# One row scatter per block at the end of attention, in a fused attention and mixture-of-experts kernel

## The chip, the cores and the metric

The kernel runs on one NeuronCore of one Trainium2 chip. The time is the device time of one execution in microseconds; the figure quoted is the median of the runs. Five engines work side by side, each through its own list of instructions in program order: TensorE (PE; its weight loads are shown apart, as PEld), VectorE (DVE), ScalarE (ACT), GpSimd (POOL) and SyncE (SP). POOL and SP also issue the DMAs.

## The reference

Two parts follow one another. The first is a gated attention over 8 sequences of 2816 tokens, whose queries and keys are the same array `z`, and whose scores go through a squared ReLU instead of a softmax:

```
scores = (1/S) * z @ z.T            # S = 2816, z has 64 columns
x = u * (max(scores, 0)**2 @ v)     # u, v: 256 columns
```

The second is a layer of 8 experts, of which each token uses one, beside a dense layer that all tokens use:

```
y = max(x @ w1_dense, 0) @ w2_dense
e = argmax(x @ w_gate);  g = softmax(x @ w_gate)[e]
y += g * (max(x @ w1[e], 0) @ w2[e])      # 256 -> 512 -> 256
```

There are 22528 tokens in all. The weights are small; which token goes to which expert is known only once its attention row is there.

## The kernel before

**Blocks.** The tokens are 176 blocks of 128. A sequence has 22 blocks. In attention, `av` (line 521) handles two blocks at a time: 22 key positions, two halves of each, and two blocks are 88 matmuls (line 548), with the score matmuls of later groups (line 383) put in between. ACT and DVE turn scores into the weights `A` (lines 398 to 413). Some of the weights are not computed but taken by DMA transpose from an earlier group (line 446, on SP). When a pair of blocks is done, DVE multiplies it by `u` and writes it to `pays` (line 577, `gate_x`), a ring of 22 blocks in SBUF. A DMA transpose of those rows (line 579) feeds the router.

**Routing and scatter.** The router works on groups of 11 blocks, at the end on groups of 8, 6, 4 and 4. `routing(q)` starts five blocks (`LAG`) after a group's last block: logits on PE (line 605), DVE's choice of expert (`route_a`), counts on PE (lines 635 and 636), and then positions in the expert's list (`route_b`), kept in `pos`. After that the blocks of the group stand in the list `waiting`. `one_scatter` takes the first of them: DVE casts the 128 positions to an index column `pi` (line 693), and POOL issues an indirect DMA that writes the block's 128 rows to the DRAM buffer `xs`, sorted by expert (line 695). This is called a row scatter below.

**The clock of the planner.** `tick(g)` runs once per block, in the middle and at the end of a pair; it does what was put down for that block with `at`, and then one row scatter. The order on PE, ACT, DVE and SP is fixed while the kernel is built, by a planner that keeps an estimated time `now` and the time at which each engine is free. For blocks after the first 154 (`Q1 * G`), `av` has a second call, in the middle of each half of a pair, so that up to two row scatters go out per block:

```
if x == nK // 2 and b * nK + i + p > Q1 * G:
    one_scatter()
```

**Tables.** When the first 14 groups (154 blocks) have their positions, `table(0)` works out, in ten steps on DVE, which rows each of the first 70 expert tiles takes, and of which expert it is. The steps are put down three to a block from block `t1` on. `table(1)` does the same for the rest, in the expert stage.

**Expert stage.** A tile is 256 rows of one expert, the last 22 are two halves of 128 rows. `fetch(s)` on SP reads a register from the table and loads the rows of `xs` by DMA transpose, then the gate and token numbers (lines 870 and 872). `expert(s)` copies that expert's weights on DVE (line 895). `slot(s)` is one step of the loop: 16 matmuls up (line 907) and 16 down (line 915), ReLU and a copy on ACT (lines 910 and 930), the weighted sum on DVE (line 931), and two scatters of finished rows to the output on POOL (line 933), called output scatters. After the first of them stands a copy on POOL that nobody reads (`pause`, line 920). DVE writes its sums in a ring of nine buffers, each of which is free when its output scatter has landed. Blocks still in `waiting` when attention ends are scattered here, one after every fifth slot, each with a pause of its own; they must all be out before the fetch of the 71st tile. The last two routing groups are routed in the first four slots.

The first three fetches are put down during the last blocks of attention, and `fetch(0)` may not start before the rows of the first 154 blocks are in `xs`. Rows of later blocks are declared independent of the first 70 tiles.

Of the kernel before, what the change touches and what calls it, by code (L numbers as in the profile page):

```python
# [19 lines left out]
def kernel(  # L20
# [19 lines left out]
    nK = S // P  # L40
    nB = N // P
    G = 11
# [5 lines left out]
    Q1 = nB // G - 2  # L48
# [35 lines left out]
    def banks(x, name, shape=(P, 2, 4 * P), dt=F32):  # L84

        return ps.tile(list(shape), dt, name=name, tag=f"b{x}")
# [179 lines left out]
    for b in range(B):  # L266
        i = 0
# [93 lines left out]
    def take_pair():  # L361
        return pairs.pop(0)[1]
# [73 lines left out]
    def far_steps(a):  # L436

        n = a + 2
        if n >= len(groups) or far[n] != [a]:
            return []  # L440
        (b, i0, w), (_, j0, wj) = groups[n], groups[a]

        def step(i):
            assert n - 1 in A
            open_group(n)
            nc.sync.dma_start_transpose(out=A[n][:, j0:j0 + wj, i * P:(i + 1) * P],
                                        in_=A[a][:, i0 + i, :wj * P])
            if i == w - 1:
                for j in range(wj):
                    key_at[n, j0 + j] = now[0] + 10.0  # L450

        return [(a, lambda i=i: step(i)) for i in range(w)]
# [68 lines left out]
    def av(n, i, between):  # L521
        b, i0, w = groups[n]
        if i == i0:
            turning.extend(far_steps(n))
        keep[0] = 0
        if n == 0 and i == i0:

            fill(n)
            for g in (0, 2):
                load_u(g, gate=True)  # L530
            need(n, 0)
        until(lambda: pairs[0][0] if pairs else None)
        ox = take_pair()
        o = banks(ox, "o")
        for p in range(2):
            rest = list(range(nK))
            for x in range(nK):
                k = rest[0]
                if i == i0 and p == 0:

                    k = min(rest, key=lambda k: (key_at.get((n, k), 9e9), k))
                    need(n, k)
                rest.remove(k)
                for h in range(2):
                    r = slice(h * dq, (h + 1) * dq)
                    j = p ^ h
                    c = (i + j - i0) * P
                    nc.tensor.matmul(out=o[:, j, 0:D], lhsT=A[n][r, k, c:c + P],  # L548
                                     rhs=v_of[b][r, k, :], start=(p == 0 and x == 0),
                                     stop=(p == 1 and x == nK - 1))  # L550
                pe(0.1092)
                keep[0] = 2 - p if x >= nK - 12 else 0
                if x % 2 == 1 and x < nK - 1:
                    fill(n)
                if x % 7 == 3 and turning:
                    t = can_turn(turning[0][0] + 2, turning[0][0])
                    if t is not None and t <= now[0] and turning[0][0] + 1 in A:
                        turning.pop(0)[1]()
                if x == nK // 2 and b * nK + i + p > Q1 * G:
                    one_scatter()  # L560
            if p == 0:
                swap_rows(n)
                between()

        def done(t):
            give_pair(t + 0.1, ox)

        g = b * nK + i
        offer(now[0] + 0.2, 0, {"dve": (0.63, lambda eng: gate_x(g, o))}, done)
        keep[0] = 0  # L570
# [13 lines left out]
    def vec(name, a, b=1, dt=F32, **kw):  # L584

        t = rt.tile([P, G * E if b > 1 else G], dt, name=name, **kw)
        return t[:, :a * b].rearrange("p (a b) -> p a b", b=b) if b > 1 else t[:, :a]
# [53 lines left out]
    def route_b(q):  # L641

        n = sizes[q]
        oh, ex, pre = rs[q]
        inc = vec("inc", E, n)

        def one():
            se = vec("se", n)
            nc.vector.tensor_reduce(out=se, in_=ex, axis=AX.X, op=ALU.add)
            o = starts[q] % (2 * G)  # L650
            rows = pays[:, o:o + n, :]
            nc.vector.reciprocal(rows.bitcast(F32)[:, :, P], se)
            nc.vector.tensor_copy(rows.bitcast(I32)[:, :, P + 1], tok[:, starts[q]:starts[q + 1]])
            assert q != Q1 or made_first[0]
            if first_of[0] != n:

                first_of[0] = n
                nc.vector.memset(smask[:, :E * n], 1.0)
                nc.vector.memset(smask[:, :E * n].rearrange("p (e t) -> p e t", e=E)[:, :, 0], 0.0)

        def two():
            tb = vec("tb", E, n)
            nc.vector.tensor_copy(tb, pre[0])
            nc.vector.tensor_add(tb[:, :, 0], tb[:, :, 0], base[:])
            nc.vector.tensor_tensor_scan(
                out=inc.rearrange("p e t -> p (e t)"), data0=smask[:, :E * n],
                data1=tb.rearrange("p e t -> p (e t)"),
                initial=0.0, op0=ALU.mult, op1=ALU.add)
            nc.vector.tensor_copy(base[:], inc[:, :, n - 1])

        def three():
            nc.vector.tensor_add(inc, inc, pre[1])
            nc.vector.tensor_mul(inc, inc, oh)
            pos = vec("pos", n, bufs=3)
            nc.vector.tensor_reduce(out=pos, in_=inc.rearrange("p e t -> p t e"),
                                    axis=AX.X, op=ALU.add)
            rs[q] = pos

        return [one, two, three]
# [179 lines left out]
    def fetch(s):  # L859

        x = take("x")
        me = mx.tile([P, 2, 2], F32, name="me", bufs=16)
        if s < NT1:
            R = nc.values_load(Rt[0][0:1, s:s + 1], engines=[ET.SP], min_val=0,
                               max_val=XROWS - T2,
                               skip_runtime_bounds_check_because="made by the table")
            xT = x.rearrange("p (c h t) -> p h c t", c=2, h=2)
            rows = xs[bass.ds(R, T2), :]
            for ins in (
                    nc.sync.dma_start_transpose(out=x.rearrange("p (c t) -> p c t", c=2),  # L870
                                                in_=rows.bitcast(BF)[:, 0:D]),
                    nc.sync.dma_start(out=me[:], in_=rows[:, P:P + 2].rearrange("(j p) c -> p j c", p=P))):

                nodep(ins, ["fx"], "xs2")
            return xT, me
        xT = x.rearrange("p (h c t) -> p h c t", c=2, h=2)
        k = 2 * (s - NT1)
        Rs = nc.values_load_multi_w_load_instructions(
            Rt[1][0:1, k:k + 2], engines=[ET.SP], min_val=0, max_val=XROWS - P,
            skip_runtime_bounds_check_because="made by the table")[1]  # L880
        for j in range(2):
            rows = xs[bass.ds(Rs[j], P), :]
            nc.sync.dma_start_transpose(out=xT[:, j], in_=rows.bitcast(BF)[:, 0:D])
            nc.sync.dma_start(out=me[:, j, :], in_=rows[:, P:P + 2])
        return xT, me
# [65 lines left out]
    got, wes = {}, {}  # L951
# [28 lines left out]
    def at(tick, fn):  # L980
        later.setdefault(tick, []).append(fn)
# [25 lines left out]
    waiting = []  # L1007
    placed = set()

    def one_scatter(dve=True):  # L1010
        if not waiting:
            return
        g = waiting.pop(0)
        if dve:
            offer(now[0], 0, {"dve": (0.1, lambda eng: scatter(g))}, lambda t: placed.add(g))
        else:
            scatter(g)
            placed.add(g)
# [47 lines left out]
    LAG = 5  # L1066
# [3 lines left out]
    for n, q in enumerate((nQ - 2, nQ - 1)):  # L1070
        at(nB + 2 * n, lambda q=q: late_routing(q))
        at(nB + 2 * n + 1, lambda q=q: late_places(q))
    t1 = Q1 * G + LAG + 2
    steps = table(0)
    for n, fn in enumerate(steps):
        at(t1 + n // 3, lambda n=n, fn=fn: offer(now[0], 0.5, {"dve": (0.7, lambda eng: fn())},
                                                 lambda t: made_first.__setitem__(0, n == len(steps) - 1)))
    fetched = [3]
    for s in range(fetched[0]):
        at(nB - 4 + s, lambda s=s: got.update({s: fetch(s)}))  # L1080
    at(nB - 2, lambda: wes.update({0: expert(0)}))
    t2 = nB + 10
    for n, fn in enumerate(table(1)):
# [21 lines left out]
    for s in range(NT - MAYBE + 2):  # L1105
        assert s + AHEAD < NT1 or not waiting
        slot(s, NT - MAYBE)
        for fn in later.pop(nB + s, []):
            fn()
        if s % 5 == 1 and waiting:  # L1110
            g = waiting[0]
            one_scatter(dve=False)
            pause(pays[:, g % (2 * G), 0:ROW].bitcast(F32))
    assert not waiting
    assert not later
    n = nc.values_load(used[0:1, 0:1], min_val=0, max_val=NH,
                       skip_runtime_bounds_check_because="made by the table")
# [34 lines left out]
```

## Time and profile before

| | |
|---|---|
| median of 3 runs | 930.4 us (929.56 to 930.82) |
| the profiled execution | 937.3 us, its span 935.5 us |
| mean granted TensorE clock | 0.987 |
| end of attention, first expert matmul | 582.7 us after the span's start |
| busy: PE, ACT, DVE, POOL | 95%, 79%, 75%, 52% of the span |
| row scatters, output scatters | 176, and 180 (40 of them for the last tiles) |

A row of the timeline gives start, duration, engine, line, operation, the tiles written and read, and in square brackets how long the engine was idle before it and what ended that. "Issue" is a wait for which the profile shows no cause, "remote" one that ended on something outside its records. A row of the windows gives the stretch and its length, the busy time and count of PE, PEld, DVE, ACT and POOL, then the granted clock, the share of the DMA engines and GB/s. A row of the waits gives who waited for whom, the total, how often, and the longest. A row of the chain gives start, length and what was running. A row of the groups gives line, engine, operation, tiles, count, busy time and mean ns, and the idle time just before it by cause.

### The profile page before, as it was taken

Reading aid. Unit: us, or ns where it says so; the run is one execution under the profiler, and the core shown is the slowest. Engines: PE = TensorE matmul, PEld = TensorE weight load, DVE = VectorE, ACT = ScalarE, POOL = GpSimd, SP = SyncE. Lnnn points to the kernel's source line nnn. Section 1 sums busy time; section 2 is a strip of 40 time slices with the busy share of each in tenths; the row PEclk is TensorE's granted clock in tenths of the full one; section 3 lists DMA queues with packets and bytes.
Section 4 is the critical chain, followed back from the end, with each engine's and each line's share of the span. In section 5 each row is a group of like instructions: output and inputs, shape, how many; then the busy total and the mean of one; then the engine's idle time right before and its main releaser. Section 6 shows DMA issues by size and latency. Waiting matters only on the chain.

```text
span 935.5 us, 30562 instructions
## 1 busy us (share of the span) xinstructions
PE 885.6 (95%) x12256; PEld 763.3 (82%) x12256; DVE 703.3 (75%) x1319; ACT 736.3 (79%) x913; POOL 489.7 (52%) x525
## 2 busy tenths in 40 slices
PE   8999999999999999999999997999899998999996
PEld 5898888888888888888887775878787887888785
DVE  6999989999999999989997972656454444446553
ACT  7999989998989989989988770667666667677664
POOL 7203343335345344344446434577777877877455
PEclk9999999999999999999999988999999999999999
DMA  7994995996997999998998745565444444434332
GB/s 139 152 181 102 164 184 112 175 200 132 178 191 133 190 179 141 193 177 142 189 188 133 140 88 91 111 123 121 100 106 106 111 111 107 117 103 95 87 91 72
DMA packets 257871, 127.64 MB, mean 136 GB/s; under 512 B 225470, under 2 KB 232894, under 8 KB 257728
## 3 DMA queue, kind: packets, MB, share of 16 engines
q1 hardware_dynamic: 230112, 70.24, 45.2%
q0 software_dynamic: 27616, 55.44, 27.7%
q8 instruction: 96, 1.57, 0.7%
q14 instruction: 47, 0.39, 0.2%
HBM read 61.54 MB, written 37.16 MB: 105 GB/s over the span
## 4 chain that ended last, share of the span: by engine, by line
PE 64%; POOL 14%; issue 12%; DVE 4%; DMA 3%; ACT 1%; POOLq 1%; SPq 0%; another core or an unknown queue 0%; DVEq 0%; ACTq 0%
PE o L548 41%; PE s L383 10%; POOL out_dram L933 9%; PE h_ps L907 6%; PE yy L915 6%; POOL zr L920 2%; DMA xT<-pays 2%; PE lg L605 1%; DVE r L400 1%; POOL A L413 1%; DVE A L413 1%; DVE ring L931 1%; DMA out_dram<-ring,ix 1%; DVE ring L895 1%; DVE pays L577 1%
## 5 line engine op out<-in xcount | busy, mean ns | idle before, releaser
L548 PE MATMUL o<-vb,A 64*128 64x256 bf16 x7744 | 501.2, 272 | 8.9 <-issue 6.0
L548 PEld LDWEIGHTS <-A 64*128 64x128 bf16 x7744 | 412.2, 95 | 62.6 <-issue 11.8
L695 POOL DMA_INDIRECT xs<-pays,pi x176 | 199.3, 1133 | 276.6 <-DVE pi L693 220.6
L398 ACT ACTIVATE r<-s 128x1024 f32<-128x1024 f32 x279 | 275.3, 1014 | 38.5 <-PE s L383 29.0
L910 ACT ACTIVATE ring<-h_ps 128x1024 bf16<-128x1024 f32 x180 | 185.6, 1032 | 95.3 <-PE h_ps L907 40.5
L411 ACT ACTIVATE A<-r 128x1024 bf16<-128x1024 f32 x252 | 256.5, 1044 | 1.7 <-DVE r L400 1.3
L413 DVE TENSOR_TENSOR A<-r 128x1024 bf16<-128x1024 f32 x172 | 208.2, 1223 | 1.1 <-ACT r L398 0.2
L931 DVE SCALAR_TENSOR_TENSOR ring<-yy,me,ring 128x256 f32<-128x256 f32 x180 | 86.1, 482 | 151.6 <-ACT ring L930 84.2
L400 DVE TENSOR_SCALAR r<-s 128x1024 f32<-128x1024 f32 (+1 forms) x153 | 185.0, 1216 | 12.3 <-PE s L383 8.3
L933 POOL DMA_INDIRECT out_dram<-ring,me x140 | 146.2, 1044 | 66.5 <-DVE ring L931 32.5
L915 PEld LDWEIGHTS <-ring 128*128 128x128 bf16 x1440 | 139.8, 98 | 38.6 <-issue 22.8
L383 PE MATMUL s<-zT 64*128 64x512 bf16 (+1 forms) x944 | 162.7, 364 | 7.1 <-remote 2.8
L915 PE MATMUL yy<-w2d,ring 128*128 128x256 bf16 x720 | 107.9, 272 | 17.3 <-DVE ring L931 15.3
L915 PE MATMUL yy<-ring 128*128 128x256 bf16 x720 | 108.0, 273 | 0.0
L907 PE MATMUL h_ps<-ring,w1d 128*128 128x256 bf16 x720 | 94.0, 273 | 3.0 <-ACT ring L910 1.3
L907 PE MATMUL h_ps<-ring 128*128 128x256 bf16 (+1 forms) x880 | 95.3, 253 | 1.4 <-issue 0.8
L895 DVE COPY ring<-wall 128x2048 bf16 x110 | 85.0, 788 | 10.4 <-issue 5.9
L930 ACT COPY ring<-yy 128x256 f32<-128x256 f32 x180 | 68.1, 378 | 30.3 <-PE yy L915 14.5
L907 PEld LDWEIGHTS <-ring 128*128 128x128 bf16 x880 | 73.4, 98 | 11.8 <-DVE ring L895 3.3
L577 DVE TENSOR_TENSOR pays<-o,ut 128x512 bf16<-128x512 f32 x88 | 61.2, 696 | 26.3 <-PE o L548 16.1
L907 PEld LDWEIGHTS <-w1d 128*128 128x128 bf16 x720 | 69.9, 98 | 12.3 <-issue 4.3
L383 PEld LDWEIGHTS <-zT 64*128 64x128 bf16 x944 | 58.5, 95 | 26.1 <-issue 15.2
(120 smaller groups left out, 359.3 us busy)
## 6 DMA issues: line engine op xcount, KB each, us to landing
ut<-in_u_dram SPq DMA_DIRECT2D x88, 256.0 KB
vb<-in_v_dram POOLq DMA_DIRECT2D x16, 384.0 KB
vb<-in_v_dram POOLq DMA_DIRECT2D x16, 320.0 KB
wall<-in_moe_w_dram POOLq DMA_DIRECT2D x16, 256.0 KB
xs<-pays,pi POOLq DMA_INDIRECT x176
zr<-in_z_dram POOLq DMA_DIRECT2D x7, 352.0 KB
out_dram<-ring,me POOLq DMA_INDIRECT x140
A<-A SPq DMA_TRANSPOSE x128
```

The source lines that it names most:

```text
L383: nc.tensor.matmul(out=s[:, h, y * c:(y + 1) * c], lhsT=zT[r, k + h, :], rhs=zT[r, i0:i0 + w, :], start=True, stop=True)
L398: nc.scalar.activation(r[:, :, :c], s[:, :, :c], AF.Relu, scale=1.0 / S)
L400: nc.vector.tensor_scalar(out=r[:, :, :c], in0=s[:, :, :c], scalar1=1.0 / S, scalar2=0.0, op0=ALU.mult, op1=ALU.max)
L411: nc.scalar.activation(a, r, AF.Square)
L413: (nc.gpsimd if eng == "pool" else nc.vector).tensor_mul(a, r, r)
L548: nc.tensor.matmul(out=o[:, j, 0:D], lhsT=A[n][r, k, c:c + P], rhs=v_of[b][r, k, :], start=(p == 0 and x == 0), stop=(p == 1 and x == nK - 1))
L695: ins = nc.gpsimd.indirect_dma_start(out=xs, out_offset=bass.IndirectOffsetOnAxis(ap=pi[:], axis=0), in_=pays[:, g % (2 * G), 0:ROW].bitca ...
L907: nc.tensor.matmul(out=h_ps[:, f, hs, :], lhsT=w1(c, f), rhs=xT[:, hs, c, :], start=(c == 0), stop=(c == 1))
L910: nc.scalar.activation(h, h_ps[:].rearrange("p f h t -> p f (h t)"), AF.Relu)
L915: nc.tensor.matmul(out=y[:, k, :], lhsT=h[:, f, j * P:(j + 1) * P], rhs=w2(f), start=(f == 0), stop=(f == 3))
L931: nc.vector.scalar_tensor_tensor(out=ys, in0=y[:, 1, :], scalar=me[:, j, 0:1], in1=yd, op0=ALU.mult, op1=ALU.add)
L933: ins = nc.gpsimd.indirect_dma_start(out=out, out_offset=bass.IndirectOffsetOnAxis(ap=ids[j], axis=0), in_=ys, in_offset=None, bounds_chec ...
```

## The change

The second call of `one_scatter` per block is taken out, so each block of attention issues one row scatter at most, to the end. What follows from it is fitted: positions of a group are kept in five buffers instead of three; the first table's steps start two blocks later; the first three fetches stand one block later, behind an assertion that the first 154 blocks have been handed to POOL; and in the expert stage the row scatters that are left go out one per three slots instead of one per five.

```
@@ in av
-                if x == nK // 2 and b * nK + i + p > Q1 * G:
-                    one_scatter()
@@ in route_b
-            pos = vec("pos", n, bufs=3)
+            pos = vec("pos", n, bufs=5)
@@ the tables and first fetches
-    t1 = Q1 * G + LAG + 2
+    t1 = Q1 * G + LAG + 4
...
+    def first_fetch(s):
+        assert not waiting or waiting[0] >= Q1 * G
+        got[s] = fetch(s)
+
     for s in range(fetched[0]):
-        at(nB - 4 + s, lambda s=s: got.update({s: fetch(s)}))
+        at(nB - 3 + s, lambda s=s: first_fetch(s))
@@ the expert stage
-        if s % 5 == 1 and waiting:
+        if s % 3 == 1 and waiting:
             g = waiting[0]
             one_scatter(dve=False)
             pause(pays[:, g % (2 * G), 0:ROW].bitcast(F32))
```

## The prediction

> **What bounds the kernel now.** I read the page's busy shares first, then windows of the attention stage, what PE waited for in each, the chain piece by piece, POOL's timeline beside it, and last the groups of the expert stage.
>
> ```profile
> PE 885.6 (95%) x12256; PEld 763.3 (82%) x12256; DVE 703.3 (75%) x1319; ACT 736.3 (79%) x913; POOL 489.7 (52%) x525
> ...
> 428.50:505.50 77.00, 76.34 (x1295) 66.85 (x1291) 71.84 (x126) 70.72 (x78) 36.87 (x35) 1.00 0.98 162
> 535.30:546.00 10.70, 6.81 (x61) 4.71 (x62) 5.50 (x14) 3.83 (x4) 5.63 (x5) 0.68 0.65 126
> 560.60:572.00 11.40, 7.11 (x112) 5.04 (x108) 1.15 (x8) 0.09 (x1) 7.61 (x8) 0.90 0.53 115
> ```
>
> TensorE is the bound almost everywhere: in the 77 us before 505.5 it is idle for 0.7. The change touches two places where that isn't so. The first is the end of attention: two windows there, 22.1 us together, have 8.2 us of PE idle, and the granted clock is 0.68 in one. The rows below say what PE waited for, first from 60 to 500 us and then from 505 to 583, and give three pieces of the chain.
>
> ```profile
> PE s L383 <- PE s L383: 2.1, 8, 0.4
> ...
> PE o L548 <- issue: 6.0, 10, 1.3
> PE s L383 <- remote: 2.8, 1, 2.8
> PE s L383 <- issue: 0.7, 1, 0.7
> ...
> 540.74 5.12 PE o L548 x48
> 557.74 3.06 PE o L548 x56
> 572.16 6.37 PE o L548 x76
> ```
>
> In 440 us of attention the longest entry is 2.1 us in all. In the last 78 us PE stood 6.0 + 2.8 + 0.7 = 9.5 us for no named engine. After two of the stalls it also ran slowly: at the 55 ns of 557.74 (3.06 / 56), the 48 matmuls would take 2.6 and the 76 take 4.2, so 2.5 + 2.2 us more are lost. Together 14.2 us. Smaller slow pieces would bring it to about 16.
>
> POOL's row scatters stand beside each stall:
>
> ```profile
> 440.12 0.99 POOL L695 DMA_INDIRECT xs<-pays,pi  x1 [0.30 <-issue]
> 512.41 0.97 POOL L695 DMA_INDIRECT xs<-pays,pi  x1 [0.30 <-issue]
> 537.90 0.97 POOL L695 DMA_INDIRECT xs<-pays,pi  x1 [0.30 <-DVE Rt L797]
> 559.82 1.76 POOL L695 DMA_INDIRECT xs<-pays,pi  x1 [10.03 <-DVE pi L693]
> 568.25 0.97 POOL L695 DMA_INDIRECT xs<-pays,pi  x1 [0.30 <-issue]
> 569.23 0.81 POOL L259 DMA_DIRECT2D wall<-in_moe_w_dram  x1
> ...
> 513.88 0.53 issue
> 537.34 2.80 another core or an unknown queue
> 565.12 0.26 issue
> 570.67 0.41 PE o L548 x2
> ```
>
> The last run is seven scatters from 559.82 to 568.25 and a weight load, spaced about 1.3 us; PE's stall begins at 565.12, after four or five of them, and ends at 570.67, 0.6 us after the load ends at 570.04. The other runs end with the scatters at 512.41 and 537.90, and PE is back at 514.41 and 540.14. The matmuls in the third stall wait for no semaphore in the program. Shorter runs did nothing: that at 440.12 closes one of three, and no wait of PE there is longer than 0.4 us. So I read it as a backlog behind a long run of scatters, whatever its channel.
>
> The second place is the expert stage, 611 to 803 us:
>
> ```profile
> L933 POOL DMA_INDIRECT out_dram<-ring,me x100 | 103.5, 1035 | 44.0 <-DVE ring L931 22.1 <-issue 17.6 <-DVE pi L693 2.5
> L920 POOL COPY zr<-ring 128x256 f32<-128x256 f32 x50 | 29.0, 580 | 0.0
> L695 POOL DMA_INDIRECT xs<-pays,pi x10 | 10.6, 1062 | 1.7 <-issue 1.7
> L920 POOL COPY zr<-pays 128x144 f32<-128x144 f32 x10 | 3.6, 363 | 0.0
> ...
> 604.26 0.87 PE yy L915 x8
> 614.15 0.98 POOL L933 DMA_INDIRECT out_dram<-ring,me  x1 [0.30 <-issue]
> 806.65 0.98 POOL L933 DMA_INDIRECT out_dram<-ring,me  x1 [0.89 <-DVE ring L931]
> 852.76 0.97 POOL L933 DMA_INDIRECT out_dram<-ring,me  x1 [0.30 <-issue]
> ```
>
> A tile's 32 matmuls cost PE 4 x 0.87 = 3.49 us. POOL's two output scatters, a pause copy and the gaps (0.30 and 0.17 in its timeline) cost 2.07 + 0.58 + 0.47 = 3.12. A row scatter with its pause adds 1.06 + 0.36 + 0.34 = 1.77. From 614.15 to 806.65 fifty tiles went by with ten row scatters: 3.85 us each. From 806.65 to 852.76 thirteen went by with none: 3.55. So one row scatter costs the stage (3.85 - 3.55) x 5 = 1.5 us, although POOL seems to have slack for it. One instance:
>
> ```profile
> 728.21 0.99 POOL L695 DMA_INDIRECT xs<-pays,pi  x1 [0.17 <-issue]
> 734.88 0.41 POOL L920 COPY zr<-ring 128x256 f32<-128x256 f32 x1
> 736.90 1.29 POOL L933 DMA_INDIRECT out_dram<-ring,me  x1 [1.62 <-DVE ring L931]
> ...
> 735.68 0.37 ACT L930 COPY ring<-yy 128x256 f32<-128x256 f32 x1 [1.17 <-PE h_ps L907]
> 736.68 0.60 PE L915 MATMUL yy<-w2d,ring 128*128 128x256 bf16 x4 [1.31 <-DVE ring L931]
> ```
>
> POOL runs dense from 728.21 to 735.29; ACT's copy then starts 1.17 us late, and PE stands 1.31 us. It looks like a small copy of the attention stall.
>
> **The change, part by part.** The profiled execution took 937.3 us, 1.8 beyond its span of 935.5, and 6.9 above the median of 930.4. The sum is made of differences and applied to the median.
>
> Removed: the second scatter per block from block 155 on. In the changed order of POOL 157 row scatters stand ahead of the first output scatter instead of 164, so seven move behind it. DVE's order has at most three between two gate products where it had five and six. By the runs above that is too few for a stall: -14.2 us, if all three go. Bounds: -16 with the small pieces; and since the timed runs are 6.9 us shorter than the profiled one, at most that much of the stalls could be absent from them, which leaves -7.3. I take -14.2: no row says the profiling made them, and the execution's surplus may lie anywhere. DVE's seven index copies are hidden beside matmuls, as the other 157 are.
>
> [...]
>
> Moved: seven row scatters into the expert stage, nineteen after its first output scatter in place of twelve, one per three tiles. POOL issues each of them and its pause; the output scatters queue behind, then DVE's product waiting for an output buffer, then PE. Price 1.5 each by the fifty tiles: +10.5. By scatters per tile, 3.85 / 2.2 and 3.55 / 2.0 both give about 1.75 per scatter, or +12.3. The low end is POOL packed without a gap, (3 x 3.12 + 1.77) / 3 = 3.71 a tile, 8 us less than now over 57 tiles. I take +10.5, measured nearest by.
>
> The first table moves two blocks later and its ten DVE steps keep their number: nothing while DVE still has scores beside it; its cover is the slack before the first fetch. Buffers for positions, five in place of three, cost no instruction.
>
> The first fetch stands one block later on SP, and now waits for block 153's scatter, whose index copy stands behind the routing step at 573.17. Behind it on SP queue the transposes for late logits and the next two fetches.
>
> ```profile
> 569.14 1.20 SPq L870 DMA_TRANSPOSE ring<-xs  x1
> 573.17 0.32 DVE L625 TENSOR_TENSOR oh<-c,m 128x48 bf16<-128x48 f32 x1
> 584.76 1.20 SPq L870 DMA_TRANSPOSE ring<-xs  x1
> ...
> 591.02 0.71 PE L907 MATMUL h_ps<-ring,w1d 128*128 128x256 bf16 x5
> DVE ring L931 <- DMA xs<-pays,pi: 2.4, 1, 2.4
> 582.70 0.38 PE h_ps L907 x2
> ```
>
> Before, the fetch left at 569.14 for matmuls at 582.70, 13.6 us. The fourth fetch left at 584.76 for matmuls at 591.02 without a stall: 6.3 us are enough. Afterwards the scatter goes at about 573.5, the fetch perhaps 2 us later, and the slow clock's 2.2 us no longer stretch the time to the first tile: about 5 us remain. I take +0.5; from 0 to +2.4, the one wait on a row scatter's landing.
>
> Sum: -14.2 + 10.5 + 0.5 = -3.2, so 930.4 - 3.2 = 927.2 us. That is 0.3% faster, above the 0.2% (1.9 us) that I take as what a measurement can tell.
>
> **The rivals.** *POOL becomes the bound of the expert stage.* Its demand per three tiles is 11.1 us against PE's 10.5, so it would stay dense, and dense running is where the 1.3 us stalls follow. If a stall adds to POOL's own time, a tile costs (11.1 + 1.3) / 3 = 4.14, 0.29 more over 57 tiles: +16.4. With -14.2 + 0.5 that is 933.1, slower. It decides from 2.2 us per moved scatter on ((14.2 - 0.5 + 1.9) / 7). Against it: in the fifty tiles the cost stayed at 1.5 us a scatter, though POOL ran dense after one there too.
>
> *The stalls stay*, the change not removing them. For it: no wait names the scatters, and two runs fall among table steps on DVE or the last transposes. Against it: three stalls, three long runs, none elsewhere. With all of them left, 930.4 + 10.5 + 0.5 = 941.4; with half, about 934. [...] No run here shows the channel, so this rival keeps its chance.
>
> *The expert stage takes the scatters for nothing or less*, PE's stalls being absorbed by POOL's backlog: +0 gives 916.7, the packed 3.71 about 909. Against it: the stage never ran packed for long.
>
> **How the numbers follow.** Forecast 0.58: its own spread, 921 to 930, lies mostly under 928.5 (0.44), else within 0.2% (0.13) or above (0.01). POOL bound 0.17, slower. Stalls stay, whole or half, 0.17, slower. Scatters free 0.08, faster. So faster 0.52, same 0.13, slower 0.35. The range runs from 916.5, which leaves half of the last case out, to 938, which leaves out the whole stalls; about 2 in 10 stand outside.
>
> **What would show it.** Right: no wait of PE above 0.6 us between 505 us and the first expert tile, granted clock 1.00 there, row scatters in runs of three at most, that tile's start some 14 us earlier than 582.7; then tiles at about 4.0 us each until the nineteenth row scatter. Wrong: stalls at the same places without a run, a tile above 4.1 us, POOL without idle time in the expert stage, or the first tile waiting for its fetch.

## The result, and the profile after

The changed kernel took 920.5 us (median of nine runs, 919.35 to 925.9) against 930.4 for the kernel before on the same chip (nine runs, 922.56 to 935.05). The ratio is 0.9923, 95% interval 0.9897 to 0.9948: faster, by more than the forecast's 0.3%. The profiled execution took 921.07 us, its span 919.0, which is 16.5 less than the profiled span of before. The line numbers of the changed kernel are two lower than those of before from the scatters on: 575 is the gate product, 693 the row scatter, 913 the second expert product, 931 the output scatter.

The end of attention first: the stretch from the gate product of blocks 154 and 155 to the last one, in windows of before and then of after (stretch, length, busy time of PE, PEld, DVE, ACT, POOL, granted clock, DMA share, GB/s).

```profile
505.54:581.96 76.42, 66.60 (x995) 52.36 (x990) 49.99 (x129) 43.62 (x49) 31.85 (x29) 0.89 0.64 114
```

```profile
502.73:563.17 60.44, 58.68 (x1011) 50.04 (x1007) 48.88 (x123) 43.88 (x49) 25.68 (x23) 1.00 0.84 137
```

It is 16.0 us shorter, PE is idle for 1.8 us of it where it was for 9.8, and the granted clock is 1.00 where it was 0.89. The waits of PE from 505 us to the first expert tile in the changed kernel (who waited for whom, the total, how often, the longest):

```profile
PE h_ps L905 <- DVE pays L575: 1.7, 1, 1.7
PE s L383 <- DVE pi L691: 0.4, 1, 0.4
PE s L383 <- ACT r L398: 0.2, 1, 0.2
```

No wait is put down to "issue" or "remote" any more; before, there were 9.5 us of them. The timeline of POOL after, where its longest run stands, and around it:

```profile
547.51 1.70 POOL L693 DMA_INDIRECT xs<-pays,pi  x1 [1.98 <-DVE pi L691]
549.51 0.97 POOL L693 DMA_INDIRECT xs<-pays,pi  x1 [0.30 <-issue]
550.78 0.97 POOL L693 DMA_INDIRECT xs<-pays,pi  x1 [0.30 <-issue]
553.33 0.96 POOL L693 DMA_INDIRECT xs<-pays,pi  x1 [1.59 <-DVE wall L253]
```

Three scatters, and no stall beside them. The first expert tile follows at once, as the timeline of DVE, PE and SP's queue has it:

```profile
563.17 0.69 DVE L575 TENSOR_TENSOR pays<-o,ut 128x512 bf16<-128x512 f32 x1 [1.74 <-PE o L548]
563.91 1.03 PE L905 MATMUL h_ps<-ring,w1d 128*128 128x256 bf16 x8 [1.67 <-DVE pays L575]
556.56 1.20 SPq L868 DMA_TRANSPOSE ring<-xs  x1
```

Its transpose went 7.35 us ahead of its matmuls, which waited for the last gate product. The tile starts 18.8 us earlier than at 582.70; 2.8 of that is there already at the gate product of block 154 (505.54 against 502.73), ahead of anything that the change touches.

The expert stage, from the first output scatter to the first one of the 70th slot, in windows of before and of after:

```profile
587.81:852.76 264.95, 247.76 (x2253) 217.74 (x2252) 136.39 (x284) 178.68 (x280) 199.70 (x232) 1.00 0.47 110
```

```profile
569.08:838.53 269.45, 248.49 (x2255) 217.62 (x2253) 134.63 (x290) 179.09 (x280) 207.33 (x246) 1.00 0.46 110
```

It is 4.5 us longer, with PE's matmuls almost unchanged. PE's largest wait in it, before and after:

```profile
PE yy L915 <- DVE ring L931: 14.0, 15, 1.8
```

```profile
PE yy L913 <- DVE ring L929: 17.2, 18, 1.6
```

So the profiles differ by -2.8 - 16.0 + 4.5, and by -2.3 in what follows the 70th slot: -16.6 for the 16.5 of the spans. The medians differ by 9.9 only. The profiled execution of before stood 6.9 us above its median, that of after 0.6 above its own.

### The profile page after: what moved, and what is told of

The parts are those of the page before. It is cut to its first block, busy times and chain, and to the rows that moved or that the text cites. A ratio compares the mean times of both kernels' runs of the same rounds, so it can differ in the third digit from the quotient of the medians.

```text
span 919.0 us, 30570 instructions
## 1 busy us (share of the span) xinstructions
PE 874.1 (95%) x12256; PEld 760.4 (83%) x12256; DVE 700.0 (76%) x1319; ACT 736.2 (80%) x913; POOL 488.8 (53%) x532
## 4 chain that ended last, share of the span: by engine, by line
PE 63%; POOL 11%; issue 10%; DMA 5%; DVE 5%; ACT 4%; SPq 1%; POOLq 1%; DVEq 0%; ACTq 0%
PE o L548 37%; PE s L383 9%; POOL out_dram L931 9%; PE h_ps L905 7%; PE yy L913 7%; ACT A L411 2%; DMA xT<-pays 2%; POOL zr L918 1%; PE lg L603 1%; ACT r L398 1%; DMA vb<-in_v_dram 1%; DVE r L400 1%; DVE A L413 1%; SPq L446 1%; DVE ring L929 1%
## 5 line engine op out<-in xcount | busy, mean ns | idle before, releaser
L548 PE MATMUL o<-vb,A 64*128 64x256 bf16 x7744 | 492.4, 270 | 2.7 <-DMA vb<-in_v_dram 1.4
L693 POOL DMA_INDIRECT xs<-pays,pi x176 | 196.5, 1117 | 271.1 <-DVE pi L691 212.6
L893 DVE COPY ring<-wall 128x2048 bf16 x110 | 80.9, 750 | 12.7 <-issue 6.1
```

What stands on the lines that cost most here:

```text
L693: ins = nc.gpsimd.indirect_dma_start(out=xs, out_offset=bass.IndirectOffsetOnAxis(ap=pi[:], axis=0), in_=pays[:, g % (2 * G), 0:ROW].bitca ...
```

## The experiments

The twelve runs went to three chips, four together on each. The kernel before takes 891.4 us on the first of them (number 6), 933.7 on the second (number 0) and 888.1 on the third (number 1). Everything below is compared within one chip, where nothing else is said. The number of the first comparison's chip is not on record, and each chip was used for one batch only, so what is called a difference between chips below could also be one between batches.

**The second scatter alone put back.** On chip 6, into the changed kernel:

```
@@ in av
+                if x == nK // 2 and b * nK + i + p > Q1 * G:
+                    one_scatter()
```

> The changed kernel with the second scatter per block put back; everything else of the change stays (table two blocks later, fetch one block later, five position buffers, left scatters one per three tiles). Theory (long runs of row scatters with no gap stop the other engines): the runs of five and more are back, and with them some 8 us or more of PE waiting for no named engine between 500 us and the first expert tile; time near 930 us, as before. Rival (the moved table or fetch freed the end of attention): no such waits, 922 us or less.

It took 885.66 us, ratio to before 0.9963 (0.9927 to 0.9999). The long runs are back, the last one in POOL's timeline:

```profile
542.60 1.76 POOL L695 DMA_INDIRECT xs<-pays,pi  x1 [8.64 <-DVE pi L693]
544.67 0.97 POOL L695 DMA_INDIRECT xs<-pays,pi  x1 [0.30 <-issue]
...
551.03 0.97 POOL L695 DMA_INDIRECT xs<-pays,pi  x1 [0.31 <-DVE pi L693]
552.00 0.81 POOL L259 DMA_DIRECT2D wall<-in_moe_w_dram  x1
553.11 0.99 POOL L695 DMA_INDIRECT xs<-pays,pi  x1 [0.30 <-DVE smask L659]
```

PE did not mind. The window of that run, and PE's two longest waits from 60 to 590 us (there is one more, of 0.3):

```profile
542.60:554.10 11.50, 11.34 (x210) 9.61 (x207) 4.23 (x20) 1.80 (x3) 9.36 (x9) 1.00 0.48 110
```

```profile
PE h_ps L907 <- DVE pays L577: 2.5, 1, 2.5
PE lg L605 <- DMA xT<-pays: 2.3, 2, 2.0
```

Neither theory had foreseen this: the runs are there and no wait on issue is, in the whole of attention. Either the other edits remove the stalls, or this chip has none.

**Bursts of six in the middle of attention.** Same chip, the changed kernel with

```
@@ in tick
-        one_scatter()
+        n = 6 if waiting and waiting[0] in (4 * G, 7 * G, 10 * G) else 1
+        for _ in range(n):
+            one_scatter()
```

> The changed kernel, but the first six row scatters of the routing groups 4, 7 and 10 are handed out in one block, in mid-attention, far from table, fetch and last transposes. Theory: at each of the three places POOL runs six scatters 1.3 us apart, and PE, ACT and DVE stop for 2 to 5 us with the clock dropping after the longer ones; 6 to 15 us in all, 926 to 935 us. Rival (the end of attention is special): no wait of PE above 0.6 us there, time as the changed kernel within 2 us, 920 us.

884.25 us, ratio 0.994 (0.9908 to 0.9972), and no wait on issue. POOL ran dense for 15, 13 and 14 transfers where the bursts are. No stall could be provoked here. The time of before, 39 us under that of the first comparison, fits a chip on which it does not happen.

**Distance between the scatters, first try.** Small copies on POOL were to stand between the scatters: in the kernel with the bursts, and in the kernel before from block 132 on.

```
+            for _ in range(6):
+                nc.gpsimd.tensor_copy(idle2[:], idle2[:])
```

> As the one with three bursts of six, with six small POOL copies between one scatter and the next. Theory: the gaps let whatever is backed up drain; no stall at the three places, time as the changed kernel, 919 to 923 us. If the number of scatters in a block matters and not their distance, it stalls as the burst does, 926 us or more.

> The kernel before, with six small POOL copies ahead of each row scatter from block 132 to the end of attention; its second scatter per block, table, fetch and one per five tiles stay. Theory: the same scatters in the same blocks but with gaps give no stall in attention, and only twelve are left for the expert stage: 4 to 7 us below the changed kernel's expert stage is not to be had, but attention should gain 10 us or more over before: 914 to 922 us. Rival (two scatters per block cost as such): 928 to 932 us as before.

They took 908.76 us (ratio 1.0199) and 926.29 (1.0366), and say nothing on distance. Nothing tied the copies to a scatter, so POOL's list had them at the kernel's start, as POOL's groups in the first 100 us of the first of them show:

```profile
L700 POOL COPY idle<-idle 128x64 f32<-128x64 f32 x108 | 26.6, 246 | 6.3
```

All 108 copies run there, ahead of weights `A` that POOL makes at that time, and in the first 110 us PE waited 21.6 us for those.

**Both kernels again, on another chip**, number 0, unchanged.

> The kernel before, unchanged, profiled on the chip that runs the next three too. Theory (long runs of scatters stop the engines, on chips that show it): stalls of PE of 6 us or more between 500 us and the first expert tile on a slow chip (about 930 us), and none on a chip where it takes under 890 us. Rival (the stalls came from one odd execution): none on either.

> The changed kernel, unchanged, on the same chip. Theory: no stall in attention on any chip; 0.8% below before where before stalls, and within 0.3% where it doesn't. Rival (the gain is in the moved table and fetch, not in stalls): the same 0.8% on any chip.

Before took 933.88 us (ratio to itself 0.9992), after 929.74 (0.9956, 0.993 to 0.9982): faster, by less than in the first comparison. PE's longest waits from 500 to 590 us, of before and then of after:

```profile
PE o L548 <- issue: 5.7, 11, 1.3
PE s L383 <- remote: 2.1, 1, 2.1
PE h_ps L907 <- DVE pays L577: 0.8, 1, 0.8
PE s L383 <- issue: 0.4, 1, 0.4
```

```profile
PE h_ps L905 <- ACT ring L908: 1.6, 1, 1.6
PE h_ps L905 <- DVE pays L575: 0.9, 1, 0.9
```

The stalls are on this chip, and with the change they are gone. From block 154 to the last gate product the windows of the two give 75.05 and 59.87 us: 15.2 less. One stall of before in the timelines of POOL and PE, merged by time:

```profile
564.64 0.97 POOL L695 DMA_INDIRECT xs<-pays,pi  x1 [0.30 <-issue]
565.92 0.97 POOL L695 DMA_INDIRECT xs<-pays,pi  x1 [0.30 <-DVE pays L577]
566.34 0.30 PE L548 MATMUL o<-vb,A 64*128 64x256 bf16 x2 [0.27 <-issue]
567.20 0.97 POOL L695 DMA_INDIRECT xs<-pays,pi  x1 [0.30 <-issue]
567.88 0.29 PE L548 MATMUL o<-vb,A 64*128 64x256 bf16 x2 [1.24 <-issue]
568.47 0.97 POOL L695 DMA_INDIRECT xs<-pays,pi  x1 [0.30 <-issue]
568.61 0.37 PE L548 MATMUL o<-vb,A 64*128 64x256 bf16 x1 [0.44 <-issue]
...
570.99 0.37 PE L548 MATMUL o<-vb,A 64*128 64x256 bf16 x1 [1.25 <-issue]
```

PE does not stop altogether: it gets one or two matmuls and then nothing for up to 1.25 us. In these two profiles what was won goes back in the expert stage, from the first output scatter to the 70th slot:

```profile
587.35:848.61 261.26, 246.95 (x2251) 217.84 (x2249) 135.78 (x283) 178.32 (x279) 200.69 (x232) 1.00 0.47 111
```

```profile
573.05:850.45 277.40, 251.47 (x2254) 218.42 (x2252) 136.56 (x290) 178.88 (x280) 207.18 (x246) 0.99 0.46 107
```

That is +16.1 us, 2.3 for each of the seven moved scatters. The second profile is the longest of the ten runs of the changed kernel (934.93, 5.2 over their median), so this is taken as an upper figure. DVE's waits on issue in these two windows, and in the same window of the first kernel of chip 6:

```profile
DVE ring L931 <- issue: 34.7, 34, 3.7
```

```profile
DVE ring L929 <- issue: 42.6, 36, 3.2
```

```profile
DVE ring L931 <- issue: 12.4, 13, 1.3
```

On chip 0 DVE too stands without a shown cause, for up to 3.7 us at a time; on chip 6 never for more than 1.3.

**Bursts of eight in the middle of attention**, same chip: as the bursts of six, with

```
+        n = 8 if waiting and waiting[0] in (2 * G, 4 * G, 6 * G, 8 * G, 10 * G) else 1
```

> The changed kernel with the first eight row scatters of the routing groups 2, 4, 6, 8 and 10 handed out in one block, in mid-attention. Theory: where before stalls on this chip, five stalls of 2 to 5 us here, 10 to 25 us above the changed kernel; where before shows none, none here, and the changed kernel's time within 3 us. Rival (something else at the end of attention stalls): none on any chip.

989.56 us, the median of four runs from 973.48 to 1002.37; ratio 1.0494 (1.0387 to 1.0601). The two shorter ones, 973.48 and 986.94, are 44 and 57 us over the changed kernel's median on this chip, far more than the 10 to 25 expected. POOL strung the five bursts together with the transfers next to them, into runs of 10, 14, 9, 10 and 13. PE's first waits from 60 to 500 us, where the profiles of before have 0.4 us on issue at most and none on remote, and the windows of two of the five places:

```profile
PE o L548 <- issue: 17.2, 32, 1.1
PE s L383 <- remote: 6.4, 2, 3.2
```

```profile
391.00:401.00 10.00, 4.57 (x29) 1.52 (x28) 3.18 (x6) 1.97 (x2) 7.35 (x8) 0.66 0.45 112
482.00:492.00 10.00, 3.38 (x19) 1.29 (x21) 1.42 (x3) 2.72 (x3) 5.57 (x6) 0.72 0.47 116
```

There PE has 29 and 19 matmuls on record in 10 us while POOL works, where the 77 us before the first stall of before have 168 in 10 us (1295 in 77), and the clock falls to 0.66 and 0.72. In the profiled execution, one of 992.18 us, the first output scatter comes at 633.5 us instead of 573.05. Long runs of scatters are thus enough to make stalls on this chip in the middle of attention too: in windows of 7 to 12 us at the five places PE is idle for 3.9, 3.5, 2.9, 5.4 and 6.6 us. Neither the table, nor the first fetch, nor the last transposes are near these places, and the edits to them are all still in.

**Distance, second try.** Same chip, the kernel before with copies that read each scatter's index, from block 143 on:

```
+        if g >= 13 * G and not late:
+            nc.gpsimd.tensor_copy(gap[:, 0:1], pi[:].bitcast(F32))
+            for _ in range(4):
+                nc.gpsimd.tensor_copy(gap[:], gap[:])
```

> The kernel before, with five small POOL copies between row scatters from block 143 to the end of attention, which push them some 1.5 us further apart. Theory: the same scatters, without stalls: 5 to 15 us below before where before stalls, and within 3 us of it where it doesn't. Rival (two scatters in a block cost as such, or fill a fixed budget): as before.

943.61 us, ratio 1.0124 (1.0032 to 1.0216). PE's waits from 500 to 600 us:

```profile
PE h_ps L913 <- DVE pays L579: 21.6, 1, 21.6
PE s L385 <- issue: 2.1, 2, 1.3
PE o L550 <- issue: 1.3, 2, 1.0
```

The waits on issue and remote fall from 8.2 to 3.4 us, and those left stand, but for one of 0.86 at 548.71, at the first run, of scatters ahead of block 143 that have no copies. But POOL is late at the end, DVE's last gate product waits behind it, and PE waits 21.6 us for that. The two later runs keep their scatters and lose nearly all of their stall, so distance helps PE in this one profile; it is no way to a faster kernel, and the timing does not separate the two effects.

**The second scatter put back, once more**, on chip 1, the same edit as the first.

> The changed kernel with the second row scatter per block put back: long runs of scatters return, all other edits (table, fetch, buffers, one row scatter per three slots) stay. If the runs cause the stalls, PE's waits on issue return in the last 80 us of attention, 6 to 10 us of them, and the first expert matmul comes about 14 us later than in the changed kernel (about 582 to 588 against 564 to 573); as about seven row scatters fewer are left for the expert stage, the total stands within 5 us of the kernel before. If the later table or fetch took the stalls away, attention ends as early as in the changed kernel and the total is 10 us or more under the kernel before. On a chip where runs of nine do nothing, none of this shows and the time is within 5 us of the kernel before.

888.36 us, ratio 0.9984 (0.9938 to 1.003). Runs of nine, six, five and nine transfers, and again no wait on issue. This chip is like number 6.

**A ladder of bursts**, same chip:

```
+        n = {2 * G: 3, 4 * G: 4, 6 * G: 5, 8 * G: 6, 10 * G: 7}.get(waiting[0], 1) if waiting else 1
```

> The changed kernel with runs of 3, 4, 5, 6 and 7 scatters back to back, in this order, in the middle of attention at groups 2, 4, 6, 8 and 10. The theory of a backlog that needs four or five says: no wait of PE on issue at the first run, one of 0.3 us or more from the third or fourth run on, growing with the length; some 20 to 40 us over the changed kernel, less than the 60 us of five runs of eight. If the time of the run, and not its length, decides (what DVE or PE do then), the stalls are unrelated to the order 3 to 7.

891.82 us, ratio 1.0041 (0.999 to 1.0091). POOL strung each burst together with the scatters and loads next to it, into runs of 5, 10, 14, 15 and 14. The window of the run of 15:

```profile
352.31:372.55 20.24, 20.24 (x342) 18.35 (x339) 19.56 (x32) 19.78 (x22) 16.57 (x15) 1.00 0.70 127
```

PE is busy for all of its 20.24 us. The length from which a stall sets in can't be read on such a chip, and is narrowed only by the other comparisons: runs of three did nothing (no wait of PE on issue from 505 us to the first expert tile in either profile of the changed kernel), runs of five and more did (9.5 us on issue and remote in the first profile of before, 8.2 in that on chip 0).

**One scatter at a time.** Same chip, bursts of eight at the five places, each index made by POOL in a single buffer:

```
+            pi = rt.tile([P, 1], I32, name="pone", bufs=1)
+            nc.gpsimd.tensor_copy(pi[:], rs[q][:, j:j + 1])
```

> Five bursts of eight scatters at the places where they cost about 60 us, but each of these scatters takes its index from a single buffer that POOL fills itself, so that it starts only when the one before has landed; as many scatters in as many bursts, at most one or two of them under way. If what stops the other engines is scatters under way at once, PE's waits on issue are under 2 us in all and the time is within 8 us of the changed kernel. If it is the number of scatters in a stretch, whatever their distance, the waits stay near 17 us and the time 40 to 60 us over the changed kernel.

929.65 us, ratio 1.047 (1.0375 to 1.0564), and no answer: the chip has no stalls to take away, and POOL's waits made new ones. DVE's two largest causes from 60 to 500 us:

```profile
DVE zn L113 <- DMA zr<-in_z_dram: 24.5, 5, 5.9
DVE pays L575 <- DMA xs<-pays,pone: 12.6, 6, 3.2
```

POOL also loads `z`, and that load stood behind scatters that waited for landings.

**The price of a row scatter in the expert stage.** Same chip, the changed kernel with nineteen more scatters there, each with its pause, into an internal buffer `xg`:

```
+        elif s % 3 == 2 and s < 58:
+            ghost(last_left[0])
+            pause(pays[:, last_left[0] % (2 * G), 0:ROW].bitcast(F32))
```

> The changed kernel with nineteen more row scatters and their pauses in the expert stage, one per three slots, which write rows of the last scatter again into a buffer that nobody reads; attention is as in the changed kernel. The price of one row scatter in the expert stage is the difference over nineteen. My forecast's 1.5 us each gives +28 us, the 0.6 us of the changed kernel's own profile +12, the 1.9 us of the same kernel on another chip +36, and nothing at all if the stage absorbs them. If POOL becomes the bound, the slots have no idle time on POOL and the price is near 1.8 each, +34.

907.29 us against 891.82 for the ladder kernel, whose expert stage is that of the changed kernel (which was not run by itself on this chip): 15.5 us, 0.8 for each. The window from the first output scatter to the 70th slot, of the ladder kernel and of this one, and this one's waits of PE there:

```profile
569.71:812.34 242.63, 242.63 (x2240) 217.55 (x2238) 134.89 (x290) 178.94 (x279) 203.74 (x246) 1.00 0.50 123
```

```profile
563.64:835.09 271.45, 255.55 (x2338) 225.55 (x2336) 140.74 (x320) 186.69 (x288) 228.99 (x284) 0.99 0.48 116
```

```profile
PE yy L922 <- DVE ring L938: 8.3, 9, 2.0
PE yy L922 <- DVE pi L700: 7.0, 7, 2.6
```

With nineteen row scatters PE is busy for the whole 242.63 us; with 38 it waits 15.3 us for DVE's ring and index columns, while DVE itself waits 58.8 us for output scatters to land. (The 271.45 are no price by themselves: POOL lags by then, and PE has done 98 matmul records of later slots inside them.) The same window with twelve scatters, in the first kernel of chip 6, and with nineteen, in the second:

```profile
564.65:807.16 242.51, 242.51 (x2240) 217.48 (x2238) 132.95 (x283) 179.07 (x279) 196.32 (x231) 1.00 0.51 120
```

```profile
563.40:805.92 242.52, 242.52 (x2240) 217.48 (x2238) 133.39 (x290) 178.94 (x279) 201.03 (x246) 1.00 0.53 123
```

Where nothing stalls, the stage takes 0.01 us more with the seven moved scatters than without.

## Why the prediction was right, and where it was off

The kernel became faster, and 920.5 lies in the range. The gain is 9.9 us by the medians where 3.2 was forecast, three times as much. On chip 0 it was 4.1, but that is no confirmation of 3.2: in the profiles there both terms of the sum were larger than forecast.

**The stalls go: right, in place and in size.** Forecast -14.2 between 7.3 and 16; the stretch shrank by 16.0 us in the first comparison and by 15.2 on chip 0. All the marks named for it are there: no wait of PE above 0.6 us before the first tile's own, the clock at 1.00, runs of three at most. The first tile came 18.8 us earlier instead of 14, 2.8 of them from ahead of the change.

**The reading that long runs make the stalls: shown on chip 0**, by the five bursts that made stalls where there had been none, and borne out by the spaced scatters. It was incomplete in that it depends on the chip: runs of nine and fifteen leave PE untouched on two others. The rival by which the stalls stay because something else makes them falls. One test is missing: the second scatter alone was put back only on the two chips without stalls, not on chip 0. What the prediction left open, the channel, is still open, and with it whether "backlog" is the right word. Beside the run of fifteen on chip 1 PE was busy for the whole 20.24 us; on chip 0 it got one or two matmuls between idle times of up to 1.25 us, which the profile puts down to issue. The packets that the DMA view counts in queues named instruction don't settle it: in the first profile of before it has none from 560 to 572 us, and PE is back from 570.67 on, so no such packet ended that stall; in the profile of before on chip 0 it has two from 558 to 572, around the stall shown, and in that of the second scatter put back on chip 6 also two, from 540 to 555, around the run that PE did not mind.

**The slow clock: right in kind.** The two quoted windows of the bursts have 0.66 and 0.72 granted where PE was idle for 5.4 and 6.6 of 10 us. That PE's idle time lowers the clock is a reading of these windows; no run shows it apart from the stalls.

**Seven row scatters in the expert stage, at 1.5 us each, +10.5: the term that was mis-sized.** It measured +4.5 in the first comparison (0.64 each), +16.1 at most on chip 0 (2.3 each) and 0.0 where nothing stalls. The step that failed is the subtraction of tiles without scatters from tiles with them: it took the difference for a fixed price of each scatter. But where nothing stalls, the stage has room for nineteen of them, and only the 38 of the last experiment used it up, at 0.8 each. What is paid on the stalling chips is then most likely the small copies of the attention stall that the prediction saw at 734.88, more of them in one execution than in another. DVE's waits on issue fit this: they grow with the change by 7.9 us on chip 0 and by 6.3 (from 40.2 to 46.5) in the first comparison. That is argued, not shown: no run took the stalls out of the expert stage on chip 0. With the measured terms of the first profile the sum is -16.0 + 4.5 = -11.5, near the 9.9 of the medians.

**The first fetch, +0.5 between 0 and 2.4: 0.** The first tile waited for the last gate product alone, with its transpose 7.35 us ahead where about 5 had been left to it.

**Tiles of about 4.0 us until the nineteenth row scatter: 3.94**, from the seventh to the 57th slot (595.77 to 792.63).

**The table and the buffers at nothing:** nothing in the waits after points to them.

**The rivals.** "Scatters for nothing", given 0.08 and 916.7 us, came nearer to the first comparison than the forecast did: 3.8 us off, against 6.7. It was near in its sum and only partly for its reason: the scatters were not free there, and the rest of the gain is stalls somewhat larger than forecast. "POOL becomes the bound" did not come true there: tiles took 3.94 us, not 4.14. In the profile on chip 0 they took 4.05, near that price, but not for that reason: POOL was busy for 207 of the 277 us there, not dense, and the medians were still 4.1 us lower than before.

**Left open:** why 930 us of before were 937 in its profile; what the change alone brings on a chip without stalls, where it wasn't timed (the changed kernel with bursts has 0.994 and 1.0041, with the second scatter 0.9963 and 0.9984, so it is probably within some 0.6%); through which channel a run of scatters holds up PE; and at which length of a run a stall begins.

## What to carry to other kernels

Where PE stands for waits that no semaphore explains, look at what POOL issues beside it: in two of the four comparisons here a run of five or more indirect DMAs without a gap cost 5 to 11 us (16.0 over three runs; 44 and 57 over five longer ones). Spreading them thinner took the stalls of attention away, 9.5 and 8.2 us of waits on issue and remote, but was free only where nothing stalled: seven more in the expert stage cost 0.01 us on one chip, 4.5 and up to 16.1 where there were stalls. Don't price a moved transfer by the mean difference between stages that have it and stages that don't: look in the waits whether the bound engine waits for it at all. Measure such a change on more than one chip before its size is believed.

## What the runs showed of the hardware that was not expected

The same kernel takes 39 to 46 us less on two of the chips (891.4 and 888.1 against 930.4 and 933.7 us), with mean granted clocks of 0.987 to 0.998 in the profiles named next. The profiled spans of the kernel before on chip 0 and of the kernel with the second scatter put back on chip 6, 929.7 and 882.4 us, show where: 22.7 of the 47.3 us lie ahead of the first output scatter (587.35 against 564.65), 18.8 from there to the 70th slot (261.26 against 242.51), 5.8 after that. Of the 22.7, 14.2 lie between the gate product of block 154 and the last one (75.05 against 60.90), where POOL's long runs stand in both, and 8.5 ahead of it, where the row scatters of before stand in runs of three at most until 503 us; why those are lost is open. The stalls of attention on chip 0 are no stops: matmuls trickle, one to five at a time; in the stall shown a group starts every 0.7 to 1.7 us, while POOL issues a scatter every 1.27.
